# The second FFN product of batches 2 to 7 as seven block products per group, by one level of Strassen's scheme

## Chip, cores, metric

The kernel runs on one core of a Trainium2 chip. The metric is the device time of one execution in microseconds (us).

## What is computed

The reference is a state exchange (an attention between 512 tokens and 32 states, in both directions) followed by a feed-forward network (FFN). Everything is float32.

```python
# x [8, 8, 512, 64], state [8, 8, 32, 64]
scores = scale * x @ state^T;   a  = softmax(scores)     # per batch and head
xread  = a @ state                                       # 512 rows per batch
scores2 = scale * state @ x^T;  a2 = softmax(scores2)
sread  = a2 @ x                                          # 32 rows per batch
y = concat([xread, sread], axis=2) -> [8 * 544, 512]     # heads side by side
h = y @ w_in                                             # [4352, 2048]
g = where(h >= 1, h, where(h <= -1, 0, (h + 1)**2 / 4))
out = g @ w_out                                          # [4352, 512]
```

## The kernel before

**Three passes for one product.** TensorE takes float32 operands here in a rounded form (fp32r). To keep the precision, each operand is split in a rounded high part and a low rest, and each product is made of three matmuls: high by high, high by low, low by high. The split costs one ACT instruction (the rounding copy) and one DVE instruction (the subtraction) for every 128x1024 tile.

**Stages of a batch.** A batch has 512 tokens. Its scores are 16 small matmuls (`scores`, L246), its softmaxes run on DVE and ACT (`second` L392, `first` L401, `halves` L410, called in program order), `trade` (L219) turns the second softmax's layout by way of DRAM on SP's queue, and `read2` (L365) makes the state rows. `a @ state @ w_in` is taken as `a @ (state @ w_in)`: `sw_pair` (L425) makes state by w_in for a 256-wide chunk of the hidden layer, and splits the result. Then come 8 units j per batch, each 256 of the 2048 hidden columns:

- `g1` (L527): the first FFN product, 12 matmuls of 128x512 (L492 to L494), into PSUM tile `h`; then the activation on ACT (`relu` L499, `square` L503) and DVE (`bound` L507), and the split of the hidden values in `gh` (ACT, L519) and `gl` (DVE, L525).
- `g2` (L538): the second FFN product, 24 matmuls of 128x512 (L556 to L558). A tile of `gh` or `gl` (128 hidden by 128 tokens) is the stationary operand, 512 columns of w_out (`wo`, high and low, resident in SBUF) the moving one; four PSUM banks `acc` collect 4 x 128 tokens over all 8 units. `store` (L564) copies them out on ACT and sends them from ACT's queue.

So a batch has 8 x (12 + 24) = 288 matmuls of 512 columns. A ninth, shorter pass (b == B) takes the 256 state rows of all batches through the same FFN.

**Order.** Batch 0, the loading and joining of the weights and a part of batch 1 are put in an order by hand: class `Plan` (L37) holds costs and dependences, the string `ORDER` gives the order of all engines, and `emit` writes it out. From batch 1 on the loop over `steps` (L838) writes the program in the order unit j's `g1`, then a part of the `g2` of unit j - 1 (`cut`, L854), then pieces of the next batch's attention, then the rest of that `g2`; each engine takes its instructions in that order.

## Time and profile before

| | |
|---|---|
| median of 3 runs | 640.94 us (640.75 to 642.06) |
| span of the profiled execution, first to last instruction | 639.1 us |
| TensorE (PE) busy | 631.2 us, 99% |
| DVE busy | 347.2 us, 54% |
| ACT busy | 355.7 us, 56% |
| DMA, mean | 83 GB/s, 53.07 MB |

The page gives the span of the profiled execution and no other time of it. PE is TensorE's matmuls, PEld its weight loads, DVE VectorE, ACT ScalarE, SP the engine that issues most DMAs. Matmuls overlap in their records: one of 512 columns is shown with 0.39 us though the next begins earlier, so the pace is read from starts, not from durations. The same holds for DVE and ACT by about 0.1 us. "<-" behind idle time names what ended it.

### The profile page before, as it was taken

What the parts mean: (1) busy time and instruction counts of PE and PEld (TensorE: products, weight loads), DVE (VectorE), ACT (ScalarE), POOL (GpSimd) and SP (SyncE); (2) the same over time, 40 slices, a digit from 0 to 9 for tenths busy, and PEclk for the clock granted to TensorE, in tenths of its full rate; (3) what the DMA queues carried; (4) which work ended last, traced back from release to release, by engine and by line L of the source; (5) the groups of instructions that cost most, each with busy time, mean ns of one, the idle gap of its engine ahead of it and who ended that gap; (6) DMA issues with size and microseconds to landing.
All of it is one profiled execution on the core that took longest, in us unless ns stands there. A gap on an engine that the chain in (4) does not pass through costs nothing.

```text
span 639.1 us, 10131 instructions
## 1 busy us (share of the span) xinstructions
PE 631.2 (99%) x4298; PEld 505.1 (79%) x4298; DVE 347.2 (54%) x494; ACT 355.7 (56%) x468; POOL 0.8 (0%) x7
## 2 busy tenths in 40 slices
PE   8999999999999999999999999999999999999997
PEld 3677787888787887888787878888787878788896
DVE  6999969433673339433773349332773244333432
ACT  6999767444654457444654456444654454544632
POOL 0000000000000000000000000000000000000000
PEclk9999999999999999999999999999999999999999
DMA  8995245000330015000420015000230012000101
GB/s 357 419 382 224 67 165 198 0 3 0 146 120 1 1 66 199 1 2 1 165 99 1 1 66 199 0 1 1 99 99 1 0 68 66 1 1 1 66 1 33
DMA packets 18476, 53.07 MB, mean 83 GB/s; under 512 B 2048, under 2 KB 7808, under 8 KB 15360
## 3 DMA queue, kind: packets, MB, share of 16 engines
q1 hardware_dynamic: 13488, 43.72, 18.4%
q10 hardware_dynamic: 4944, 8.72, 3.7%
q8 instruction: 33, 0.54, 0.3%
q14 instruction: 11, 0.09, 0.0%
HBM read 38.80 MB, written 13.63 MB: 82 GB/s over the span
## 4 chain that ended last, share of the span: by engine, by line
PE 93%; DMA 3%; DVE 1%; ACT 1%; issue 0%; SPq 0%; ACTq 0%
PE acc L556 19%; PE acc L557 19%; PE acc L558 19%; PE h L492 10%; PE h L493 10%; PE h L494 10%; PE sw L435 4%; DMA raw_o<-in_moe_w_out_dram 2%; PE sr L373 1%; DMA raw_i<-in_moe_w_in_dram 1%; PE sc L264 1%; DVE sw_3l L451 0%; DVE s L297 0%; DVE sw_1l L451 0%; ACT raw_i L602 0%
## 5 line engine op out<-in xcount | busy, mean ns | idle before, releaser
L556 PE MATMUL acc<-wo,gh 128*128 128x512 f32 x544 | 212.9, 391 | 0.0
L557 PE MATMUL acc<-wo,gh 128*128 128x512 f32 x544 | 212.0, 390 | 0.0
L558 PE MATMUL acc<-wo,gl 128*128 128x512 f32 x544 | 211.8, 389 | 0.0
L501 ACT ACTIVATE u<-h,half 128x512 f32<-128x512 f32 (+1 forms) x129 | 91.9, 712 | 174.7 <-PE h L494 163.5
L509 DVE SCALAR_TENSOR_TENSOR u<-u,h 128x512 f32<-128x512 f32 (+1 forms) x129 | 86.6, 710 | 181.2 <-ACT u L505 181.1
L556 PEld LDWEIGHTS acc<-wo,gh 128*128 128x128 f32 x544 | 102.1, 188 | 24.9 <-issue 3.3
L558 PEld LDWEIGHTS acc<-wo,gl 128*128 128x128 f32 x544 | 102.1, 188 | 21.4
L557 PEld LDWEIGHTS acc<-wo,gh 128*128 128x128 f32 x544 | 102.1, 188 | 21.0 <-DVE wo L629 0.2
L525 DVE TENSOR_TENSOR gl<-u,gh 128x1024 fp32r<-128x1024 f32 (+1 forms) x69 | 83.4, 1209 | 53.9 <-ACT gh L519 53.9
L519 ACT CAST gh<-u 128x1024 fp32r<-128x1024 f32 (+1 forms) x69 | 71.6, 1037 | 66.4 <-DVE u L509 65.3
L505 ACT ACTIVATE u<-u 128x1024 f32<-128x1024 f32 (+1 forms) x69 | 72.4, 1049 | 1.8
L435 PE MATMUL sw<-w,sb 64*32 64x256 f32 x1024 | 32.3, 380 | 1.4 <-DVE w L618 1.0
L435 PEld LDWEIGHTS sw<-w,sb 64*32 64x32 f32 x1024 | 18.1, 106 | 10.8 <-DVE u L509 2.1
L571 ACT COPY o<-acc 128x512 f32<-128x512 f32 x33 | 19.0, 583 | 12.1 <-PE acc L558 12.1
L492 PE MATMUL h<-ath,sw_5h 128*128 128x512 f32 x64 | 25.1, 391 | 0.0
L492 PE MATMUL h<-ath,sw_3h 128*128 128x512 f32 x64 | 25.0, 390 | 0.0
L493 PE MATMUL h<-ath,sw_5l 128*128 128x512 f32 x64 | 24.9, 390 | 0.0
L494 PE MATMUL h<-atl,sw_3h 128*128 128x512 f32 x64 | 24.9, 390 | 0.0
L493 PE MATMUL h<-ath,sw_3l 128*128 128x512 f32 x64 | 24.9, 389 | 0.0
L494 PE MATMUL h<-atl,sw_5h 128*128 128x512 f32 x64 | 24.9, 389 | 0.0
L492 PE MATMUL h<-ath,sw_1h 128*128 128x512 f32 x60 | 24.4, 407 | 0.0
L493 PE MATMUL h<-ath,sw_1l 128*128 128x512 f32 x60 | 23.4, 391 | 0.0
(163 smaller groups left out, 693.1 us busy)
## 6 DMA issues: line engine op xcount, KB each, us to landing
xt<-in_xt_dram SPq DMA_DIRECT2D x16, 512.0 KB, 4.2
raw_i<-in_moe_w_in_dram SPq DMA_DIRECT2D x8, 1024.0 KB, 10.7
raw_o<-in_moe_w_out_dram SPq DMA_DIRECT2D x8, 1024.0 KB, 14.7
xn<-in_x_dram SPq DMA_DIRECT2D x8, 1024.0 KB, 5.8
out_dram<-o ACTq DMA_DIRECT2D x32, 256.0 KB, 2.0
e_x<-e_there SPq DMA_DIRECT2D x32, 128.0 KB, 2.9
e_there<-e SPq DMA_DIRECT2D x7, 512.0 KB, 2.6
e_there<-e SPq DMA_DIRECT2D x2, 256.0 KB, 2.8
```

The source lines that it names most:

```text
L435: nc.tensor.matmul(banks[hh][pr * NS:(pr + 1) * NS, cols], lhsT=sb[rows, b, pr], rhs=w32[c][rows, pr], start=True, stop=True,)
L492: nc.tensor.matmul(o, lhsT=wh[:, k, sl], rhs=ah[:, k], start=first, stop=False)
L493: nc.tensor.matmul(o, lhsT=wl[:, k, sl], rhs=ah[:, k], start=False, stop=False)
L494: nc.tensor.matmul(o, lhsT=wh[:, k, sl], rhs=al[:, k], start=False, stop=last)
L501: nc.scalar.activation(out=u, in_=h, func=AF.Relu, scale=0.5, bias=half)
L505: nc.scalar.activation(out=u, in_=u, func=AF.Square)
L509: nc.vector.scalar_tensor_tensor(out=u, in0=u, scalar=1.0, in1=h, op0=ALU.min, op1=ALU.max)
L519: nc.scalar.copy(out=gh, in_=u)
L525: nc.vector.tensor_tensor(out=gl, in0=u, in1=gh.bitcast(F32), op=ALU.subtract)
L556: nc.tensor.matmul(a, lhsT=lh, rhs=oh, start=f == 0, stop=False)
L557: nc.tensor.matmul(a, lhsT=lh, rhs=ol, start=False, stop=False)
L558: nc.tensor.matmul(a, lhsT=ll, rhs=oh, start=False, stop=f == NF - 1)
```

## The change

Batches 0 and 1 and the state rows keep the second product as it was. Batches 2 to 7 are taken in three pairs, and the second product of a pair is made in two groups, one for each half (1024) of the hidden columns: six groups g = 0 to 5. In a group the product is `out^T = w^T g`, with the weights as stationary operand and 512 tokens as moving one. The operands are cut in 2 x 2 blocks: the weights in two halves of the 512 output columns and two interleaved halves of the hidden columns, the hidden values in the two interleaved halves and the two batches of the pair. By one level of Strassen's scheme (in Winograd's form) seven block products k = 1 to 7 take the place of eight. One block product is four `quarter`s of 6 matmuls of 128x512, so a group has 168 matmuls where it had 192.

The scheme needs sums of blocks:

- **Sums of weights.** `block_ops(c)`, for each of 8 chunks: DVE makes the whole weight from its parts and four sums, ACT and DVE split the sums, and SP writes the four plain and the four summed blocks (1 MB each) to DRAM. `weight_ops(g, k)` loads the block of one product (1 MB, in pieces of 1 KB) from DRAM to SBUF; there are two such buffers ("wt"), and 7 loads in each of six groups.
- **Sums of hidden values.** `operand_ops(g, k, half)`: DVE makes the sum in place (T, for k = 5, 6, 7, 4), then ACT and DVE split the operand in `hi` and `lo`, in one of three buffers ("win"). Two operand tiles per product, 14 per group, where there were 8 splits in two half batches.
- **Sums of results.** `done_ops`: a product's PSUM pair is copied (ACT) or added (DVE) into an SBUF tile. Two chains of products go on in PSUM (A: k = 1, 6, 7, 4; B: k = 5, 3), and the next product of the chain waits for the copy. Odd groups add to the result of the even group before and send it, transposed, from SP's queue. The host turns the rows of batches 2 to 7 back (`_rows`).

The loop over `steps` is gone. A second planner, class `Flow`, takes every step from batch 1's first unit on with a cost and dependences; PE's order is written out in the program, and the order on ACT, DVE and SP is made by list scheduling (the step that can begin first, of those the one due first). A whole hidden unit is one `bound` instead of two. PSUM is one tensor of four two-bank pairs, dealt out by the planner; most large SBUF tiles are slots at fixed addresses. The last two `g2` units of batch 1 are put between the first units of batch 2. At the end, the state rows' pass reads w_out back from DRAM (`last_weights`), 8 loads of 1 MB.

The diff, cut to its core (the `Flow` class and the allocation are left out):

```diff
@@
+        flow.kinds.update({kd: ("pair", n) for kd, n in (("base", 6), ("win", 3), ("wt", 2), ("out", 2), ("wo", 8), ("g10", 1), ("spare", 1))})
...
+        flow.kinds.update({kd: ("pb", n) for kd, n in (("h", 4), ("sw", 4), ("sc", 4), ("sr", 4), ("acc", 4), ("A", 1), ("B", 1))})
...
+            op(("dA", c), "SP", 2.6, lambda: store_block(0, rounded(wo_at[c]).bitcast(F32)), [("wol", c)], ends=[("wo", c)])
+            op(("wa", c), "DVE", 1.14, whole, [("wol", c), ("send", 0, 3)], take=[("s", ("s", c))], ends=[("wo", c)])
+            op(("ws", c), "DVE", 1.5, sums, [("wa", c)])
+            op(("wsh", c), "ACT", 0.97, sum_high, [("ws", c)])
+            op(("wsl", c), "DVE", 1.14, sum_low, [("wsh", c)])
+            op(("dS", c), "SP", 2.6, lambda: store_block(1, place()), [("wsl", c)], ends=[("s", c), "spare", "spare2"])
...
+        BLOCK = {1: 0, 2: 2, 3: 7, 4: 3, 5: 4, 6: 5, 7: 6}
+        HOME = {1: (0, 0), 2: (0, 1), 3: (1, 1), 4: (1, 0), 5: (1, 0), 6: (1, 0), 7: (0, 0)}
+        CHAIN = {1: "A", 6: "A", 7: "A", 4: "A", 5: "B", 3: "B", 2: "C"}
...
+            if k == 5:
+                op(("T", g, 1, half), "DVE", 1.14, lambda: tt(s2(), s2(), s1(), ALU.subtract),
+                   blocks_of[homes[0]] + blocks_of[homes[1]])
+                need = [("T", g, 1, half)]
...
+            op(("hi", g, k, half), "ACT", 0.97, lambda: nc.scalar.copy(out=view()[:, 0], in_=value()), need,
+               take=[("win", win)], ends=ends)
+            op(("lo", g, k, half), "DVE", 1.14,
+               lambda: tt(view()[:, 1], value(), view()[:, 0].bitcast(F32), ALU.subtract), [("hi", g, k, half)], ends=ends)
...
+                part, n = divmod(BLOCK[k], 4)
+                nc.sync.dma_start(
+                    out=rounded(flow.place[h]).bitcast(F32).rearrange("p (c f) -> p c f", f=CI),
+                    in_=blocks[g % 2, part].rearrange("p c (e k f) -> p (c e) k f", e=2, k=4)[:, :, n],
+                )
...
+            op(h, "SP", 2.6, fetch_block, [("dA" if BLOCK[k] < 4 else "dS", 4 * (g % 2) + c) for c in range(4)],
+               take=[("wt", h)])
...
+        def quarter(g, k, n):
...
+                for d in range(2):
+                    o = chain(g, k)[:, d]
+                    wh, wl = (w[:, n, e, d * P:(d + 1) * P] for e in range(2))
+                    for m, (lhs, e) in enumerate(((wh, 0), (wl, 0), (wh, 1))):
+                        nc.tensor.matmul(
+                            o, lhsT=lhs, rhs=v[:, e, a], start=fresh and n == m == 0, stop=n == 3 and m == 2,
+                            skip_group_check=not fresh,
+                        )
...
+            if n == 0 and k in (6, 7, 3, 4):
+                need.append(({6: "X", 7: "Y", 3: "V", 4: "C22"}[k], g))
...
+            add = odd or name in ("C12", "C22", "C11")
...
+                if add:
+                    nc.vector.tensor_tensor(out=c, in0=c, in1=src, op=ALU.add)
+                else:
+                    nc.scalar.copy(out=c, in_=src)
...
+        for j, (k, n) in enumerate(((1, 0), (1, 2), (2, 0), (2, 2))):
+            step(0, k, n)
+            step(0, k, n + 1)
+            unit_ops(3, j)
+        for g in range(5):
+            b, j0 = 2 + (g + 1) // 2 * 2, 4 * ((g + 1) % 2)
+            both(b, j0)
+            read_ops(3 + g)
+            if 4 + g < B:
+                score_ops(4 + g)
+            ks = (5, 6, 3, 7, 4) if g == 0 else (1, 5, 6, 3, 7, 2, 4)
+            places = (0, 3, 5, 8, 10, 13, 16, 18) if g == 0 else (2, 5, 9, 12, 16, 19, 23, 26)
+            middle = 9 if g == 0 else 14
+            line = [(k, n) for k in ks for n in range(4)]
+            for n in range(len(line) + 1):
+                if n in places:
+                    i = places.index(n)
+                    unit_ops(b + i // 4, j0 + i % 4)
+                if n == middle:
+                    both(b + 1, j0)
+                if n < len(line):
+                    step(g, *line[n])
+        sread_ops()
+        line = [(k, n) for k in (1, 5, 6, 3, 7, 2, 4) for n in range(4)]
+        for n, q in enumerate(line):
+            if n in (16, 22):
+                last_unit((16, 22).index(n))
+            step(5, *q)
```

Here `unit_ops` is the first product and activation of one unit, `both` makes two `sw_pair`s of two chunks each, `read_ops` is `read2`, `score_ops` is the attention of one batch, and `step` is `weight_ops`, `operand_ops` and `quarter` of a product's quarter n.

## Rows read from the trace of the kernel before

**Rows 1.** The page's head and busy times (us, share of the span, instructions).

```profile
span 639.1 us, 10131 instructions
PE 631.2 (99%) x4298; PEld 505.1 (79%) x4298; DVE 347.2 (54%) x494; ACT 355.7 (56%) x468; POOL 0.8 (0%) x7
```

**Rows 2.** The page's chain that ended last, by engine.

```profile
PE 93%; DMA 3%; DVE 1%; ACT 1%; issue 0%; SPq 0%; ACTq 0%
```

**Rows 3.** The same chain in order of time: start us, us, what.

```profile
165.25 1.03 PE sr L373 x64
166.28 1.89 PE sw L435 x64
168.17 0.86 PE sc L264 x16
...
236.68 1.03 PE sr L373 x64
```

**Rows 4.** Timeline of PE: start us, us, line, out<-in, shapes.

```profile
171.13 0.39 PE L492 MATMUL h<-ath,sw_1h 128*128 128x512 f32 x1
...
171.81 0.39 PE L556 MATMUL acc<-wo,gh 128*128 128x512 f32 x1
...
177.25 0.39 PE L492 MATMUL h<-ath,sw_1h 128*128 128x512 f32 x1
```

**Rows 5.** Windows, one batch: PE, PEld, DVE, ACT, POOL busy; clock; DMA share; GB/s.

```profile
236.68:308.11 71.43, 71.43 (x500) 57.52 (x504) 36.57 (x56) 37.40 (x51) 0.00 (x0) 1.00 0.17 60
```

**Rows 6.** Timeline of DVE while it runs without a break.

```profile
49.08 1.22 DVE L618 SCALAR_TENSOR_TENSOR w<-raw_i 128x1024 int32<-128x1024 int32 x1
50.21 0.68 DVE L284 TENSOR_REDUCE m<-z 128x16 f32<-128x512 f32 x1
50.81 1.22 DVE L525 TENSOR_TENSOR gl<-u,gh 128x1024 fp32r<-128x1024 f32 x1
```

**Rows 7.** Timeline of ACT while it runs without a break.

```profile
39.56 1.03 ACT L519 CAST gh<-u 128x1024 fp32r<-128x1024 f32 x1
40.50 1.05 ACT L625 CAST wo<-wf 128x1024 fp32r<-128x1024 f32 x1
```

**Rows 8.** Windows of 20 us: two of the stage with a list schedule, one later.

```profile
40.00:60.00 20.00, 20.00 (x116) 15.76 (x115) 19.19 (x23) 19.94 (x23) 0.00 (x0) 1.00 0.83 316
60.00:80.00 20.00, 20.00 (x117) 15.93 (x116) 19.50 (x25) 16.11 (x20) 0.00 (x0) 1.00 0.18 53
...
240.00:260.00 20.00, 20.00 (x99) 16.25 (x87) 18.33 (x33) 12.20 (x20) 0.00 (x0) 1.00 0.46 159
```

**Rows 9.** The page's DMA issues: KB each, us to landing.

```profile
raw_i<-in_moe_w_in_dram SPq DMA_DIRECT2D x8, 1024.0 KB, 10.7
raw_o<-in_moe_w_out_dram SPq DMA_DIRECT2D x8, 1024.0 KB, 14.7
xn<-in_x_dram SPq DMA_DIRECT2D x8, 1024.0 KB, 5.8
...
e_x<-e_there SPq DMA_DIRECT2D x32, 128.0 KB, 2.9
e_there<-e SPq DMA_DIRECT2D x7, 512.0 KB, 2.6
```

**Rows 10.** Windows of 1 us: a trade's reads in 1 KB pieces, then xn.

```profile
250.00:251.00 1.00, 1.00 (x6) 0.81 (x6) 0.96 (x3) 0.22 (x1) 0.00 (x0) 1.00 0.87 264
251.00:252.00 1.00, 1.00 (x6) 0.84 (x5) 0.97 (x3) 0.86 (x2) 0.00 (x0) 1.00 0.94 215
...
253.00:254.00 1.00, 1.00 (x6) 0.84 (x5) 1.00 (x3) 1.00 (x3) 0.00 (x0) 1.00 1.05 418
```

**Rows 11.** Timeline of PE, first stage: waits in brackets.

```profile
13.29 0.67 PE L435 MATMUL sw<-w,sb 64*32 64x256 f32 x16 [0.99 <-DVE w L618]
...
17.41 0.67 PE L435 MATMUL sw<-w,sb 64*32 64x256 f32 x16 [0.45 <-DVE sw_0l L451]
```

**Rows 12.** Timeline of DVE: the kernel's last compute instruction.

```profile
635.07 0.69 DVE L569 COPY o<-acc 128x512 f32<-128x512 f32 x1 [5.42 <-PE acc L558]
```

More of the change, by code (lines that the diff above doesn't have):

```diff
@@ L18 @@
 WARM = 7
-PAD = 120
+PAD = 96
+UNITS = 27
 EARLY = (2, 3)
@@ L263, in scores @@
                         m = m[:, half]
[L264 to L266 removed]
+                    nc.tensor.matmul(o, lhsT=sb[rows, b, pr], rhs=m, start=True, stop=True)
         def tokens(self, half):
@@ L918, in _laid_out, with _rows @@
     }
+def _rows(y):
+    y = y.copy()
+    for b in range(2, 8):
+        y[b * 544:b * 544 + 512] = y[b * 544:b * 544 + 512].T
+    return y
 def kernel(**inputs):
```

782 lines of the change are left out of this document (611 added, 171 removed).

## Prediction

> **What bounds the kernel now.** The first look is at the busy times and the span [rows 1]: TensorE (PE) is busy for 631.2 of 639.1 us, the other engines for a little over half of it. A busy PE need not be at its pace, so the second look is at the chain that ended last [rows 2, 3]: 93% of it is PE, and in the steady batches it goes from one PE instruction to the next, with nothing between. The third is at the starts on PE's timeline [rows 4]: a `g2` unit of 24 matmuls runs from 171.81 to 177.25, so 5.44 / 24 = 0.2267 us each, and the `g1` matmuls ahead of it keep the same pace (0.68 / 3). The fourth is at a batch [rows 5]: 71.43 us from one `read2` to the next [rows 3], PE without a gap at clock 1.00, DVE 36.57 us and ACT 37.40 us. The sum agrees: 288 x 0.2267 + 1.03 + 1.89 + 1.89 + 0.86 [rows 3] = 70.96, and 0.47 us for the changes between kinds of matmul. So every PE instruction that goes is worth its full pace, as long as nothing else comes to be late; DVE has 35 us free in each batch, ACT 34.
>
> **What is removed.** Each of the six groups has 24 matmuls of 128x512 fewer: 144 x 0.2267 = 32.6 us. The new ones have the shape and the operand kinds of `g1` (128x128 stationary, 512 moving), whose pace is the same [rows 4]. The median, 640.94, stands 1.84 us above the span, and no other time of that execution is shown; I leave those 1.84 us as they are and make the sum on the median: 640.94 - 32.64 = 608.3 us, if PE never waits. The first stage (up to unit 0 of batch 1) and the tail behind PE (a 0.69 us copy and a DMA, 639.1 - 635.07 = 4.0 us [rows 12]) stay. The Trainium skill ("TensorE: Matmul & The Clock Gate", in "Wait — 56ns, not 53.3ns?") has a warm matmul start every N / 2.4 GHz plus 2.5 ns, 215.8 ns here, by which the gain would be 31.1 us. The trace disagrees for these fp32r matmuls, and its 226.7 ns is what I use.
>
> **What DVE gets.** DVE's price is read from starts too: behind a 128x1024 instruction the next begins after 1.13 us, behind a 512 one after 0.60 [rows 6]. A batch period of before becomes one turn of the loop over g, with 65.99 us of PE (71.43 - 5.44). DVE's 36.57 us get 8 sums T and 6 more `lo` splits, and result adds: 7 in an odd group, 3 in an even one. Loops 1 and 3: 36.57 + 21 x 1.13 = 60.3 us, 91% of 65.99. Loop 2: 17 more, 55.8 us, 85%. Loop 0 has only 20 quarters (20 x 1.36 + 8 x 2.72 + 6.14 = 55.1 us of PE) and 12 more instructions, 50.1 us, 91%. Loop 4 has no attention and lies well below. The weight sums lie in batch 1's stage of some 115 us: 8 chunks x (2 x 1.13 + four quarter-size sums). Four of those cost between one full instruction (1.13) and four half ones (2.4); I take 1.5, so 30 us (27 to 37), on top of 0.51 x 115 = 59 us. DVE is under 85% there, and they cost nothing. The merged `bound` saves under 0.1 us each and is left out. ACT: 6 more roundings and up to 4 copies at 0.94 us [rows 7], less four output copies: under 47 us of 65.99. It doesn't bind.
>
> So DVE is nowhere over 100%, and the question is whether 91% can be filled without PE waiting. One stretch of the trace shows it: the stage that is already in a list-scheduled order has DVE at 19.19 and 19.50 of 20 us (ACT at 19.94 in the first), and PE at 20.00 in both [rows 8]. The operands have slack as well. An operand's buffer comes free three tiles ahead, four quarters and a unit (8.16 us) before its use, and making it takes 0.94 + 1.13 us and two hand-overs. I take nothing for DVE's load as such.
>
> **PSUM pairs.** At the start of a turn two `sw_pair`s, `read2`, scores and the fresh chain A take five pairs in 3.8 us, where four exist. The first to come back is the first `sw_pair`'s, 0.95 + 0.94 + 1.13 us and three hand-overs after its start, some 3.3 us if DVE is free at once and 4.5 if it has just begun another 1024 instruction. Chain A then waits between 0 and 1.2 us. The two `sw_pair`s in the middle of a turn meet a like squeeze. Ten places x 0 to 1.2 us: 0 to 12; I take 0.25 each, 2.5 us, since in several of the ten the last hidden unit's pair is back in time.
>
> **The weight stream.** A load of 1 MB begins when the product before the last frees its buffer, and must land within one product. Pieces of 1 KB ran at 264 GB/s with the DMA engines 0.87 busy and at 215 with 0.94 [rows 10], so 303 to 215 GB/s at full use, 3.5 to 4.9 us. To this comes the fixed part: `e_there`, 512 KB in 2.6 us, leaves 1.35 us beyond its 1.25 at 418 GB/s; `xn`, 1 MB in 5.8, leaves 3.3, but stands behind `e_x` [rows 9, 10]. Bounds 4.8 to 8.2 us. I take 5.7 (240 GB/s and 1.35), since a load whose buffer has just come free is alone as `e_there` is. In loops 0 to 4 a product has at least one hidden unit beside its four quarters: 5.44 + 2.72 = 8.16 us, so the load is hidden. In group 5 three products (k = 5, 6, 3) have 5.44 us alone: 3 x 0.3 = 0.9 us (0 to 8.3). The output DMAs go from ACT's queue to SP's, and the trades, `xt` and `xn` share SP's queue with the loads. A load that waits there for its buffer holds them back, but what they feed (`kept`, `read2`, the next scores) is used a turn later. The 16 stores of 1 MB lie in batch 1, where the DMA engines are 0.17 busy over a batch [rows 5]. The eight loads of w_out at the end have buffers freed 10 us or more before their use, at nothing.
>
> **Sum.** 608.3 + 2.5 + 0.9 = 611.7 us. Its own range: 608 to 619.
>
> **The rivals.**
>
> *DVE becomes the bound.* In the loop that was written by hand DVE's best stretch is 18.33 of 20 us [rows 8]; a full turn at 91% with chains DVE - ACT - DVE in it is not in the trace, and rows 8 stand for 40 us, not 250. If DVE can be filled to only 0.85, loops 0, 1 and 3 take 58.9, 70.9 and 70.9 us: 13.6 us more than PE's, 625 us. If it is under 0.80, the four loops take 226.5 / 0.80 = 283 us against PE's 253.1, and the whole gain is gone: that is the case on the other side, slower than before, and 0.80 is where it decides (0.75 gives 661 us).
>
> *The weights come late.* With a load of L us, loops 1 to 4 pay 28 x (L - 9.43) and group 5 7 x (L - 7.0); the forecast's gain of 29.2 us is gone at L = 9.8. For it: in the first stage 1 MB took 10.7 to 14.7 us [rows 9], and 10.7 gives 61 us more, 673 us. Against it: there many loads stood in one queue with the DMA engines 0.83 busy and more [rows 8]. The Trainium skill ("DMA: Bandwidth & Descriptors", "Latency and other measured facts") says that copies between HBM tensors whose partitions lie a large power of two apart run at 103 to 207 GB/s, from a pitch of 512 KiB up. The stored blocks have a pitch of 32 KiB, which it does not list; no run here shows it yet. At its 103 GB/s, an estimate, a load would take 11.5 us, and this rival would be the outcome.
>
> *The planner's waits aren't the program's.* With one PSUM tensor and overlapping SBUF views, waits may be written between steps that don't touch the same bytes, and PE would wait before each quarter. In the first stage a `sw_pair` waited for its operand 0.45 to 0.99 us [rows 11]; 168 quarters x 0.45 = 76 us, 688 us, and 0.17 us per quarter takes the gain. Nothing in the steady rows shows such a wait.
>
> **How the numbers follow.** Forecast (608 to 619 us) 0.62. DVE at 0.80 to 0.89 (619 to 640 us) 0.22, most of it below 630. DVE below 0.80, 0.05; late weights, 0.05; waits at the quarters, 0.05: all slower. Within 0.2%, which is about what a measurement of this kernel can tell from no change, 0.01. So faster 0.84, same 0.01, slower 0.15. The range 608 to 630 leaves out the slower cases and the end of the DVE case, 0.2 in all.
>
> **What would show it.** 4154 or so matmuls, with starts 0.2267 us apart in the quarters. One turn of loops 1 to 3 in 66 to 67 us, PE at 19.8 or more of 20, DVE at 17 to 18. Waits of PE at the starts of turns, on DVE's `sw` split or the last result, up to 1 us each. In group 5 PE waits of some 0.3 us on DMA, at products 5, 6 and 3. Weight loads landing in 5 to 7 us. The clock stays 1.00. Wrong it is if PE's waits are on `lo`, T or a result add through the whole of loops 0 to 3 (DVE), on the weight loads (stream), or before quarters whose operands have long been there (waits). If PE's pace in the quarters is not 0.2267 us, the first step fails.

## The result, and the profile after

The changed kernel takes **620.58 us** (median of 4 runs, 619.43 to 621.72) against 640.88 (640.75 to 642.06) for the kernel before: a ratio of 0.968, with a 95% interval of 0.9666 to 0.9694. The forecast was 611.7 us with a range of 608 to 630. So the direction and the range held, but 8.9 us of the gain that was forecast didn't come, and this part is about where they went.

The head of the page of after and its chain by engine (compare [rows 1, 2]):

```profile
span 618.8 us, 10012 instructions
PE 602.2 (97%) x4154; PEld 477.1 (77%) x4154; DVE 497.5 (80%) x574; ACT 391.3 (63%) x480; POOL 0.8 (0%) x7
...
PE 82%; DVE 10%; DMA 4%; ACT 3%; issue 1%; SPq 0%; DVEq 0%
```

There are 144 matmuls fewer, as said. In the profiled executions the sum of the prediction gives a span of 639.1 - 32.64 = 606.5 us if PE never waits; the span is 618.8. So 12.3 us were lost, where the prediction had put 3.4. The chain that ended last has 10% of DVE in it where it had 1%: PE waits for DVE somewhere. The windows by stage say where (length; PE, PEld, DVE, ACT, POOL busy; clock; DMA share; GB/s). The first is batch 1's stage, then come loop 0 and the turns of loops 1 to 3:

```profile
84.30:208.50 124.20, 119.06 (x920) 92.64 (x918) 102.77 (x141) 77.51 (x103) 0.00 (x0) 0.99 0.66 246
208.54:267.42 58.88, 55.69 (x425) 43.66 (x424) 49.70 (x57) 41.23 (x52) 0.00 (x0) 1.00 0.43 143
267.42:333.58 66.16, 66.16 (x474) 52.85 (x473) 57.70 (x65) 41.14 (x52) 0.00 (x0) 1.00 0.57 183
333.58:399.73 66.15, 66.15 (x473) 52.84 (x473) 55.99 (x63) 42.95 (x54) 0.00 (x0) 1.00 0.51 168
399.73:465.88 66.15, 66.15 (x473) 52.84 (x472) 57.70 (x65) 41.26 (x52) 0.00 (x0) 1.00 0.53 168
```

The turns of loops 1 to 3 run as forecast: 66.15 us each (65.99 forecast), PE without a gap though DVE is 85 to 87% busy. Batch 1's stage and loop 0 don't: PE is idle for 5.1 and 3.2 us there. The prediction had put the first at nothing and the second's share at half a microsecond. The waits themselves stand in brackets on PE's timeline (start us, us, instruction, idle before and what ended it). These are all of them from batch 1's stage on:

```profile
95.89 1.09 PE L455 MATMUL bank<-xt,sb 64*32 64x512 f32 x16 [0.54 <-DVE sw_1l L621]
129.02 0.67 PE L605 MATMUL bank<-w,sb 64*32 64x256 f32 x16 [0.88 <-DVE one L681]
134.16 0.50 PE L664 MATMUL bank<-ath,sw_5h 128*128 128x512 f32 x1 [0.50 <-DVE sw_7l L621]
154.23 1.96 PE L605 MATMUL bank<-w,sb 64*32 64x256 f32 x32 [2.43 <-DVE sw_0l L621]
186.56 3.02 PE L1261 MATMUL bank<-r,r 128*128 128x512 f32 x12 [0.80 <-DVE f L681]
211.74 1.10 PE L569 MATMUL bank<-xn,one 128*32 128x64 f32 x64 [1.24 <-DVE f L681]
215.14 0.50 PE L664 MATMUL bank<-ath,sw_4h 128*128 128x512 f32 x1 [1.17 <-DVE sw_6l L621]
240.33 1.10 PE L605 MATMUL bank<-w,sb 64*32 64x256 f32 x32 [0.74 <-DVE f L681]
500.41 1.10 PE L605 MATMUL bank<-w,sb 64*32 64x256 f32 x32 [0.36 <-DVE f L681]
```

They add up to 8.66 us: 5.15 in the stage, 3.15 in loop 0, 0.36 in loop 4. In eight of the nine the waiting work is one of the small products (`sw_pair` at L605, `read2` at L569, scores at L455) or the first matmul of a hidden unit (L664) behind small products. No quarter in loops 1 to 4 or in group 5 waits.

The longest wait can be followed step by step on three engines: PE's first `sw_pair`, ACT's rounding, DVE's subtraction, PE's second `sw_pair`.

```profile
150.70 1.09 PE L605 MATMUL bank<-w,sb 64*32 64x256 f32 x32
...
151.91 1.01 ACT L619 CAST sw_0h<-bank 128x1024 fp32r<-128x1024 f32 x1 [0.17 <-PE bank L605]
...
152.95 1.23 DVE L621 TENSOR_TENSOR sw_0l<-bank,sw_0h 128x1024 fp32r<-128x1024 f32 x1 [0.53 <-ACT sw_0h L619]
```

One PSUM pair goes through the whole chain before the second `sw_pair` can begin at 154.23: 3.53 us from start to start. The prediction had priced this chain at 3.3 us, but saw a need for it at the starts and middles of turns alone. Here two `sw_pair`s stand back to back in PE's order while four banks still collect batch 1's output, so that of the four pairs only two are dealt out to everything else, and one of these was in use.

Behind this wait PE was slow as well. Windows of 1 us, with the granted clock as the third number from the right:

```profile
154.00:155.00 1.00, 0.77 (x16) 0.45 (x24) 0.70 (x2) 1.00 (x2) 0.00 (x0) 0.60 0.00 0
155.00:156.00 1.00, 1.00 (x24) 0.22 (x8) 1.00 (x2) 0.40 (x1) 0.00 (x0) 0.50 0.00 0
156.00:157.00 1.00, 1.00 (x10) 0.79 (x3) 0.83 (x1) 0.70 (x1) 0.00 (x0) 0.50 0.60 254
157.00:158.00 1.00, 1.00 (x4) 0.76 (x4) 0.66 (x1) 0.31 (x1) 0.00 (x0) 0.69 0.95 401
```

The clock fell to 0.50, the lower of its two levels (1.2 of 2.4 GHz), and came back by 158. The `sw_pair` of 154.23 took 1.89 us to the next matmul where others take 1.02, and the four matmuls from 156.12 to 157.83 took 1.71 where four take 0.91: 1.67 us more. Waits and low clock together are 10.3 of the 12.3 us.

Of the DMA groups the new ones are (KB each, us to landing; compare [rows 9]):

```profile
r<-blocks SPq DMA_DIRECT2D x50, 1024.0 KB, 5.5
...
blocks<-r SPq DMA_DIRECT2D x8, 1024.0 KB, 10.5
```

A weight load lands in 5.5 us (5.7 forecast). The stores of plain blocks take 10.5.

### The profile page after: what moved, and what is told of

It is laid out like the page before. It is cut to its first block, busy times and chain, and to the rows that moved or that the text cites. A ratio compares the mean times of both kernels' runs of the same rounds, so it can differ in the third digit from the quotient of the medians.

```text
span 618.8 us, 10012 instructions
## 1 busy us (share of the span) xinstructions
PE 602.2 (97%) x4154; PEld 477.1 (77%) x4154; DVE 497.5 (80%) x574; ACT 391.3 (63%) x480; POOL 0.8 (0%) x7
## 3 DMA queue, kind: packets, MB, share of 16 engines
q1 hardware_dynamic: 65040, 121.32, 55.8%
## 4 chain that ended last, share of the span: by engine, by line
PE 82%; DVE 10%; DMA 4%; ACT 3%; issue 1%; SPq 0%; DVEq 0%
PE bank L1261 37%; PE bank L664 9%; PE bank L666 9%; PE bank L665 9%; PE bank L717 4%; PE bank L719 4%; PE bank L718 4%; PE bank L605 3%; DMA blocks<-f 1%; DMA f<-in_moe_w_in_dram 1%; DMA e_there<-one 1%; DVE one L681 1%; DVE w L778 1%; PE bank L455 1%; PE bank L569 1%; DVE r L696 1%
## 5 line engine op out<-in xcount | busy, mean ns | idle before, releaser
L1261 PE MATMUL bank<-r,r 128*128 128x512 f32 x1008 | 238.9, 391 | 0.8 <-DVE f L681 0.8
L1261 PEld LDWEIGHTS bank<-r,r 128*128 128x128 f32 x1008 | 188.4, 188 | 44.6 <-issue 2.1
L673 ACT ACTIVATE f<-bank,half 128x512 f32<-128x512 f32 x104 | 71.7, 689 | 107.2 <-PE bank L666 106.4
L1203 DVE TENSOR_TENSOR r<-f,r 128x1024 fp32r<-128x1024 f32 x84 | 101.6, 1218 | 9.1 <-ACT r L1227 8.9
L1227 ACT CAST r<-f 128x1024 fp32r<-128x1024 f32 x84 | 87.0, 1046 | 27.6 <-PE bank L1261 13.4
L681 DVE SCALAR_TENSOR_TENSOR f<-f,bank 128x1024 f32<-128x1024 f32 x52 | 63.2, 1216 | 38.1 <-ACT f L677 37.8
L717 PE MATMUL bank<-r,r 128*128 128x512 f32 x160 | 63.1, 395 | 0.0
L718 PE MATMUL bank<-r,r 128*128 128x512 f32 x160 | 62.6, 391 | 0.0
L719 PE MATMUL bank<-r,r 128*128 128x512 f32 x160 | 62.6, 391 | 0.0
L677 ACT ACTIVATE f<-f 128x1024 f32<-128x1024 f32 x52 | 55.2, 1061 | 1.3
L1295 DVE TENSOR_TENSOR one<-one,bank 128x1024 f32<-128x1024 f32 x30 | 36.4, 1214 | 14.5 <-PE bank L1261 14.5
L1203 DVE TENSOR_TENSOR f<-f,f 128x1024 f32<-128x1024 f32 x36 | 43.3, 1216 | 0.0
L605 PE MATMUL bank<-w,sb 64*32 64x256 f32 x1024 | 34.0, 388 | 5.9 <-DVE sw_0l L621 2.9
L717 PEld LDWEIGHTS bank<-r,r 128*128 128x128 f32 x160 | 30.3, 189 | 8.5 <-issue 1.2
L719 PEld LDWEIGHTS bank<-r,r 128*128 128x128 f32 x160 | 30.2, 189 | 6.4
L718 PEld LDWEIGHTS bank<-r,r 128*128 128x128 f32 x160 | 30.2, 189 | 6.1
L605 PEld LDWEIGHTS bank<-w,sb 64*32 64x32 f32 x1024 | 17.3, 108 | 19.3 <-issue 4.6
L681 DVE SCALAR_TENSOR_TENSOR one<-one,bank 128x1024 f32<-128x1024 f32 (+1 forms) x17 | 19.6, 1155 | 2.3 <-ACT one L677 2.2
L664 PE MATMUL bank<-ath,sw_0h 128*128 128x512 f32 x52 | 20.5, 394 | 0.0
## 6 DMA issues: line engine op xcount, KB each, us to landing
blocks<-r SPq DMA_DIRECT2D x8, 1024.0 KB, 10.5
```

The source lines that it names most:

```text
L605: nc.tensor.matmul(banks[hh][pr * NS:(pr + 1) * NS, cols], lhsT=sb[rows, b, pr], rhs=w32[c][rows, pr], start=True, stop=True,)
L664: nc.tensor.matmul(o, lhsT=wh[:, k, sl], rhs=ah[:, k], start=first, stop=False)
L673: nc.scalar.activation(out=u, in_=h, func=AF.Relu, scale=0.5, bias=half)
L681: nc.vector.scalar_tensor_tensor(out=u, in0=u, scalar=1.0, in1=h, op0=ALU.min, op1=ALU.max)
L717: nc.tensor.matmul(a, lhsT=lh, rhs=oh, start=f == 0, stop=False)
L718: nc.tensor.matmul(a, lhsT=lh, rhs=ol, start=False, stop=False)
```

## The experiments

All times are medians of 4 runs, each beside runs of the kernel before on the same chip (medians of 640.75 to 640.88 us).

### Why PE waits in batch 1's stage and in loop 0

Three theories. **A**: small products ask for a PSUM pair before one is back, because of their place in PE's order. **B**: DVE is overfull with the sums of weights. **C**: DVE stands for a buffer that is still being stored, and what is queued behind it comes late.

**The sums left out.**

```diff
+            def both_stores():
+                for first in range(2):
+                    store_block(first, rounded(wo_at[c]).bitcast(F32))
-            op(("dA", c), "SP", 2.6, lambda: store_block(0, rounded(wo_at[c]).bitcast(F32)), [("wol", c)], ends=[("wo", c)])
-            op(("wa", c), "DVE", 1.14, whole, [("wol", c), ("send", 0, 3)], take=[("s", ("s", c))], ends=[("wo", c)])
-            op(("ws", c), "DVE", 1.5, sums, [("wa", c)])
+            op(("dA", c), "SP", 2.6, both_stores, [("wol", c)], ends=[("wo", c)])
+            op(("wa", c), "DVE", 1.14, lambda: None, [("wol", c), ("send", 0, 3)], take=[("s", ("s", c))], ends=[("wo", c)])
+            op(("ws", c), "DVE", 1.5, lambda: None, [("wa", c)])
...
```

> Left out: DVE's and ACT's instructions for the sums of the weights (some 30 us of DVE in batch 1's stage); the second set of stores sends the plain weights again, so DRAM traffic and all orders stay. The changed kernel stands 12.3 us above the sum of PE's work, 8 to 9 of it in batch 1's stage (84 to 209 us), 3 to 4 in loop 0, in eight waits of PE at the small products (state by w_in, scores, read2), the longest 2.43 us at 151.8 us with the clock at its lower level behind it. Theory A (these products ask for a pair of PSUM banks before one is back, because of where they stand in PE's order): the waits shrink where a late DVE held the pair, but don't go: 614 to 618 us. Theory B (DVE is overfull with the sums): the waits of batch 1's stage go, 611 to 613 us. Theory C (DVE stands still for the stores, as at 121.7 us for 3.4 us, and is late from there on): without sums nothing waits for a store, so also 611 to 613 us; the next run tells B from C.

Measured: 621.54 us (620.93 to 622.53), ratio 0.9702 (0.9687 to 0.9716). Nothing was gained. The window with the longest wait, and the wait on PE's timeline:

```profile
140.00:160.00 20.00, 17.57 (x128) 13.26 (x127) 7.85 (x7) 10.53 (x12) 0.00 (x0) 0.94 0.32 121
```

```profile
157.01 1.39 PE L605 MATMUL bank<-w,sb 64*32 64x256 f32 x32 [2.43 <-DVE sw_0l L621]
```

DVE is busy for 7.85 of 20 us here, and the wait is 2.43 us as before, to the hundredth. An engine that is free for 60% of the time isn't overfull: B falls. The waits of 0.50, 0.80 and 0.88 us went, but the 16 stores now come as soon as the weights are split, and a trade waits behind them (DVE's timeline, then PE's):

```profile
122.81 1.25 DVE L551 STREAM_TRANSPOSE one<-e_x 128x1024 f32<-128x1024 f32 x1 [8.70 <-DMA e_x<-e_there]
...
126.56 0.50 PE L717 MATMUL bank<-r,r 128*128 128x512 f32 x1 [2.15 <-ACT r L690]
```

What was gained at the small waits was lost at 126 us, and the clock fell to 0.50 behind this wait as well. The sums of weights had spread the stores out.

**Half of the stores left out.**

```diff
-            op(("dS", c), "SP", 2.6, lambda: store_block(1, place()), [("wsl", c)], ends=[("s", c), "spare", "spare2"])
+            op(("dS", c), "SP", 2.6, lambda: None, [("wsl", c)], ends=[("s", c), "spare", "spare2"])
...
-                part, n = divmod(BLOCK[k], 4)
+                part, n = 0, BLOCK[k] % 4
```

> Left out: the eight stores of the summed weights (8 of 16 MB); the loads of summed blocks read plain blocks in the same pieces. DVE's and ACT's work and all orders stay. Theory C: DVE no longer stands still for 3.4 us for a buffer that is being stored, and the waits of batch 1's stage go: 611 to 614 us. Theory B: DVE has the same work, no change beyond 2 us: 618 to 621 us. Theory A: as B, at most 2 to 3 us less where the late DVE held a pair: 617 to 621 us.

Measured: 618.66 us (617.62 to 619.97), ratio 0.9662 (0.9646 to 0.9678), 1.9 us below the changed kernel. The waits of 0.88, 0.50 and 0.80 us (2.2 together) are gone and one of 0.49 has come; the 2.43 us and all of loop 0's stay. So C is right for about 2 us, and no more. In the changed kernel it is seen on DVE's timeline:

```profile
125.02 1.23 DVE L1167 TENSOR_TENSOR f<-r 128x1024 f32<-128x1024 f32 x1 [3.36 <-DMA blocks<-f]
```

DVE's next instruction in its queue, a whole-weight sum, waits 3.36 us for a store to leave its buffer, and the `bound` queued behind it hands back its pair late (L681 on DVE ends the 0.88 us of 129.02).

**Only two lines of PE's order.**

```diff
         unit_ops(1, 7)
-        g2_half(1, 5, 0)
         sw_make((2, 0), (2, 1))
-        sw_make((2, 2), (2, 3))
+        g2_half(1, 5, 0)
         g2_half(1, 5, 1)
+        sw_make((2, 2), (2, 3))
         unit_ops(2, 0)
```

> All work as in the changed kernel; only two lines of PE's order in batch 1's stage change places: the first sw_pair of batch 2 goes one half unit earlier, the second one half unit later, so that they no longer stand back to back. Theory A (a sw_pair asks for its PSUM pair before ACT and DVE have handed one back, because of its place): the 2.43 us wait at 154 us goes, and a new one of at most 0.4 us at another place comes; 620.6 - 2.4 + 0.4 = 618.6 us if the lower clock behind that wait (0.50 to 0.60 from 154 to 157 us) stays, and 1.3 to 1.8 us less, 617 us, if the low clock is a consequence of the wait. Theory D (the low clock at 154 us has another cause, such as the DMA load of that stretch): the low clock stays near 154 us in the windows of 1 us. Theory C (DVE stands for the stores): the waits come back elsewhere in the stage, and the time stays at 620 to 621 us.

Measured: 617.79 us (615.6 to 618.34), ratio 0.9632 (0.9614 to 0.9651). A window, and a wait on PE's timeline:

```profile
140.00:160.00 20.00, 20.00 (x143) 15.33 (x142) 19.86 (x26) 14.79 (x17) 0.00 (x0) 1.00 0.44 186
```

```profile
131.03 0.67 PE L605 MATMUL bank<-w,sb 64*32 64x256 f32 x16 [2.79 <-DVE one L681]
```

The 2.43 us wait is gone without another in its neighbourhood, with DVE at 19.86 of 20 us, and the clock is 1.00: with the wait, the low clock is gone. The DMA load, which theory D named, isn't its cause: with the sums left out the clock fell behind the same wait while no DMA ran.

```profile
158.00:159.00 1.00, 1.00 (x10) 0.58 (x3) 0.63 (x1) 0.55 (x1) 0.00 (x0) 0.50 0.00 0
```

But the wait doesn't always bring the clock down. With half of the stores left out the same 2.43 us are followed by a clock of 1.00, and from this `sw_pair` to the next matmul 1.02 us pass, not 1.89:

```profile
153.03 1.10 PE L605 MATMUL bank<-w,sb 64*32 64x256 f32 x32 [2.43 <-DVE sw_0l L621]
```

```profile
153.00:154.00 1.00, 0.97 (x32) 0.50 (x32) 0.73 (x1) 1.00 (x2) 0.00 (x0) 1.00 0.00 0
```

The wait of 0.80 us at 186 went as well. What wasn't expected is the row of 131.03: the wait that had been 0.88 us at 129 is 2.79 here. The planner had put DVE's and SP's steps in another order even before 131 us, and DVE stood 5.27 us for a store where it had stood 3.36. By the rows: 2.43 + 1.67 + 0.80 saved, 1.91 given back, 3.0; measured 2.8.

**The small products moved apart in the whole stage.** Work and planner are unchanged. Lines of PE's order change places, the lines of `block_ops` come to stand between them, and the planner orders ACT, DVE and SP anew (the first lines of the edit):

```diff
-        unit_ops(1, 0)
-        for n in range(2):
-            g2_half(0, 7, n)
-        for c in range(NC):
-            block_ops(c)
         sw_make((1, 1), (1, 2))
-        sw_make((1, 3), (1, 4))
-        read_ops(0)
+        unit_ops(1, 0)
+        g2_half(0, 7, 0)
+        g2_half(0, 7, 1)
+        block_ops(0)
+        block_ops(1)
+        block_ops(2)
         score_ops(2)
...
```

> Only PE's order in batch 1's stage (84 to 209 us) is changed: the same small products (state by w_in, read2, scores) stand apart from one another, between the halves of the big products. DVE, ACT and DMA have the same work, list-scheduled by the same rule. Theory A: the waits of that stage go, and the lower clock with them: 611 to 614 us; loop 0 keeps its waits. Theories B and C: the work of DVE and the stores are what they were, so 617 to 621 us.

Measured: 616.06 us (615.83 to 616.56), ratio 0.9616 (0.9601 to 0.963), 4.5 us below the changed kernel. Of the stage's 5.15 us of waits 0.38 is left, and the clock is 1.00 throughout.

**The same in loop 0 as well.** In the order of loop 0 `read2` goes first, the two middle `sw_pair`s stand apart and two units go elsewhere:

```diff
+            if g == 0:
+                read_ops(3)
+                sw_make((2, 4), (2, 5))
+                sw_make((2, 6), (2, 7))
+                score_ops(4)
+                unit_ops(2, 4)
...
+                sw_make((3, 4), (3, 5))
+                unit_ops(2, 7)
...
+                sw_make((3, 6), (3, 7))
...
```

> As e4_moved_stage, and the small products of loop 0 are moved apart in the same way. Theory A: loop 0's 3 to 4 us go too, 608 to 611 us, PE's work being 608.3 us by the sum. Theories B and C: 616 to 621 us.

Measured: **614.15 us** (613.33 to 614.75), ratio 0.9584 (0.957 to 0.9598), 6.4 us below the changed kernel. These waits are left:

```profile
134.56 0.50 PE L664 MATMUL bank<-ath,sw_5h 128*128 128x512 f32 x1 [1.60 <-DVE sw_5l L621]
...
208.08 1.09 PE L455 MATMUL bank<-xt,sb 64*32 64x512 f32 x16 [0.21 <-DVE f L681]
209.44 0.50 PE L664 MATMUL bank<-ath,sw_4h 128*128 128x512 f32 x1 [0.27 <-DVE sw_4l L621]
...
494.27 1.10 PE L605 MATMUL bank<-w,sb 64*32 64x256 f32 x32 [0.36 <-DVE f L681]
```

So A is shown for the larger part: with no work taken away and only the order changed, 6.2 of the 8.66 us of waits and the low clock go. Of the stage's waits up to 2.2 us can be put down to C as well, since they also went when stores were left out. The 2.43 us, which two lines removed, and loop 0, whose waits stayed when stores were left out, are A's alone.

### How much DVE can take

The prediction's first rival was that DVE can't be filled to 91% without PE waiting. The turns of 66.15 us say that it can; how far it goes is measured by giving DVE more work.

**Half of each `lo` split done twice, and the whole of it.**

```diff
-            op(("lo", g, k, half), "DVE", 1.14,
-               lambda: tt(view()[:, 1], value(), view()[:, 0].bitcast(F32), ALU.subtract), [("hi", g, k, half)], ends=ends)
+            def low():
+                tt(view()[:, 1], value(), view()[:, 0].bitcast(F32), ALU.subtract)
+                tt(view()[:, 1, 0], value()[:, 0], view()[:, 0, 0].bitcast(F32), ALU.subtract)
+
+            op(("lo", g, k, half), "DVE", 1.14, low, [("hi", g, k, half)], ends=ends)
```

> Nothing is left out; behind each of the 14 lo splits of a group DVE repeats one half of it (128x512, 0.60 us), 8.4 us more of DVE in a group, at nothing for PE. In the three full turns DVE was busy 57.70, 55.99 and 57.70 of 66.15 us; now it has 66.1, 64.4 and 66.1. Theory F (DVE's share costs nothing up to 100%): the turns stay within 0.5 us of 66.15, and the whole within 2 us of 620.6. Rival G (a loop with chains between DVE and ACT can be filled to 95% only): turns of 69.6, 67.8 and 69.6 us, 8.5 us more, 629 us. Rival H (the prediction's rival, 0.85 to 0.87): turns of 76, 74 and 76 us, 648 us.

> Nothing is left out; DVE does each of the 14 lo splits of a group twice (128x1024, 1.13 us), 15.8 us more of DVE in a group: 73.5, 71.8 and 73.5 us of DVE work for turns in which PE has 66.15. Theory F (only what is over 100% costs): the turns take DVE's time, 73.5, 71.8 and 73.5 us, 20.4 us more; loop 0 (49.7 us of DVE in 58.9, 11 to 14 more) 2 to 4 us more; group 5 and loop 4 up to 5 us more: 643 to 650 us, slower than before. Theory G (95%): turns of 77.4, 75.6 and 77.4 us, 32 us for these alone, 655 us and more. If PE's time doesn't follow DVE's, 630 us or less, then what is queued on DVE isn't what PE waits for.

Measured: 645.18 us (643.85 to 645.34) with the half repeats, 24.6 us more than the changed kernel and 0.6% above the kernel before (ratio 1.0061, 1.0046 to 1.0076); 667.87 us (667.05 to 671.16) with the full ones, 47 us more. F falls as it was put: with the half repeats the first full turn takes 71.54 us, though DVE is busy for only 67.11 of them. A turn has two halves, divided by its second pair of `sw_pair`s. The changed kernel's first full turn in halves, then the same with the half repeats, cut at the same `sw_pair`, and PE's wait behind the cut:

```profile
267.42:301.50 34.08, 34.08 (x277) 26.98 (x276) 33.40 (x42) 22.00 (x30) 0.00 (x0) 1.00 0.59 186
301.50:333.58 32.08, 32.08 (x198) 25.87 (x197) 24.30 (x24) 19.14 (x22) 0.00 (x0) 1.00 0.55 181
```

```profile
273.24:308.02 34.78, 34.17 (x277) 26.96 (x276) 34.47 (x45) 20.59 (x29) 0.00 (x0) 1.00 0.56 182
308.02:344.78 36.76, 33.85 (x197) 26.60 (x197) 32.64 (x35) 20.79 (x24) 0.00 (x0) 0.95 0.48 154
```

```profile
312.03 1.47 PE L605 MATMUL bank<-w,sb 64*32 64x256 f32 x32 [2.91 <-DVE f L681]
```

In the changed kernel DVE is busy for 33.40 of 34.08 us in the first half, 98%, and for 76% of the second: the mean of 87% hid a half with 0.7 us to spare. On DVE's timeline seven of the 14 splits of the turn stand in the first half, so the half repeats add 7 x 0.60 = 4.2 us to it, 3.5 more than there was room for. PE's waits up to the second `sw_pair` behind the cut are 0.61 and 2.91 us, 3.52 together: DVE is busy for 99% of the time up to the cut, its queue runs on behind it, and that `sw_pair` stands for a pair whose `bound` comes late in the queue. The rest of the 5.38 us by which the turn grew lies behind this wait, where the clock fell to 0.50.

**Six repeats in the second half only.** New theory K: each half is a unit of its own.

```diff
+            def low():
+                again = g in (1, 2, 3) and k in (2, 4) or g in (2, 3, 4) and k == 1
+                for _ in range(2 if again else 1):
+                    tt(view()[:, 1], value(), view()[:, 0].bitcast(F32), ALU.subtract)
```

> Nothing is left out; DVE repeats six lo splits (128x1024, 1.13 us) in each of loops 1 to 3, those that fall into the second half of a turn (products 2 and 4, and product 1 of the next group): 6.8 us more of DVE in a turn, against the 8.4 us of the half repeats, which were spread over the whole turn and made a turn 5.4 to 5.9 us longer. In the changed kernel DVE had 33.40 of 34.08 us in the first half of a turn (up to its second pair of sw_pairs) and 24.30 of 32.08 in the second; now it has 33.4 and 31.1. Theory K (each half of a turn is a unit of its own: the sw_pairs between them wait for DVE's queue, so that DVE's work costs nothing up to 100% of a half and its full time beyond): turns within 0.5 us of 66.15 and 620.6 us for the whole, though DVE is busy 64.5 of 66.15 us, 97%. Rival G (DVE can be filled to a share of a whole turn only, 92% by the half repeats: 66.1 of 71.5 us): 64.5 / 0.92 = 70.1 us for a turn, 12 us more in three turns, 632 us.

Measured: 620.81 us (619.53 to 621.57), ratio 0.9684 (0.9669 to 0.9699): no change.

```profile
268.33:302.41 34.08, 34.08 (x277) 26.97 (x276) 33.40 (x42) 22.00 (x30) 0.00 (x0) 1.00 0.56 186
302.41:334.49 32.08, 32.08 (x197) 25.85 (x196) 31.61 (x30) 19.14 (x22) 0.00 (x0) 1.00 0.51 159
```

DVE is busy for 65.01 of 66.16 us, 98% of the turn, and PE never waits. K holds and G falls: 6.8 us of DVE work cost nothing in one half of the turn, while 8.4 us spread over both cost 5.4 to 5.9 us a turn.

### The weight stream

```diff
-                nc.sync.dma_start(
-                    out=rounded(flow.place[h]).bitcast(F32).rearrange("p (c f) -> p c f", f=CI),
-                    in_=blocks[g % 2, part].rearrange("p c (e k f) -> p (c e) k f", e=2, k=4)[:, :, n],
-                )
+                for _ in range(2):
+                    nc.sync.dma_start(
+                        out=rounded(flow.place[h]).bitcast(F32).rearrange("p (c f) -> p c f", f=CI),
+                        in_=blocks[g % 2, part].rearrange("p c (e k f) -> p (c e) k f", e=2, k=4)[:, :, n],
+                    )
```

> Nothing is left out; each 1 MB weight load is issued twice into the same buffer by SP, one behind the other, so that a product's weights are there only when 2 MB have landed. One load took 5.5 us to landing; the second adds 2.5 (418 GB/s) to 4.9 us (215 GB/s): 8.0 to 10.4 us. Theory S (the stream was hidden, with what a product takes as its margin: 8.16 us and more in loops 1 to 4, 5.44 to 9.4 us in group 5): the turns stay at 66.2 us if the load takes under 8.2 us, and group 5 loses 7 x (L - 7.0), 7 to 24 us; 628 to 645 us, with PE waits on the weight buffer in group 5. Rival W (late weights already cost something in the loops): the turns grow by 7 x (L - 9.43) only above L = 9.43, so with L = 10.4 by 6.8 us each, 28 us more in the loops as well. If neither grows, the real margin is larger than the formulas of the prediction have it: the load then starts earlier than when the product before the last ends.

Measured: 717.97 us (716.76 to 722.87), 97 us more, far outside what was expected. The dose was not the intended one: the second load goes into the same buffer, and SP waits with it until the first has landed. The waits of PE and of SP's queue (us in total, times, longest):

```profile
PE bank L1262 <- DMA r<-blocks: 50.9, 16, 9.3
...
SPq L1238 <- DMA r<-blocks: 321.1, 42, 13.7
```

SP waited 321.1 / 42 = 7.6 us for each first load, and 7.2 us is the page's median for all loads, to landing: together some 14.8 us, not 8.0 to 10.4. So this run shows that late weights would have taken the whole gain, as that rival had it, and not how large the margin is. By the prediction's formula 14.8 us would have cost 7 x (14.8 - 9.43) = 38 us in each turn; the first turns grew from 66.15 to 82.4, 86.1 and 77.8 us, half of that or less. How much later than 5.5 us a load may land stays open.

### What is left

**Another order, with units moved in all loops.** The small products and hidden units stand at other places in the stage and in loops 0 to 4, and most `sw_pair`s stand alone among quarters (some 230 lines of order):

```diff
+        sw_make((4, 2), (4, 3))
+        read_ops(4)
+        step(1, 1, 0)
+        step(1, 1, 1)
+        score_ops(5)
+        sw_make((4, 0), (4, 1))
+        step(1, 1, 2)
...
```

> The same work as in the changed kernel; PE's order is another in batch 1's stage and in loops 0 to 4: the sw_pairs, read2, scores and hidden units stand at other places, apart from each other. Theory A: the waits for PSUM pairs in the stage and in loop 0 (8 us with the lower clock behind them in the changed kernel, of which the order that moved only the small products took 6.4) go but for some 1 us, and the 0.36 us at 500 us too: 612 to 614 us. Theory C (what is left are stands of DVE for stores in batch 1's stage): 1.5 to 3 us of waits stay between 120 and 160 us. If the order with moved units brings operands too late, new waits on lo, T or hi stand in the loops and the time is above 614.2 us.

Measured: 615.59 us (615.47 to 616.06), ratio 0.9606 (0.9592 to 0.9621). The windows of 20 us from batch 1's stage on have PE at 20.00, but for one:

```profile
204.00:224.00 20.00, 19.48 (x191) 14.97 (x180) 19.55 (x23) 14.18 (x19) 0.00 (x0) 1.00 0.67 211
```

That is a wait of 0.52 us, and no other is left in the stage or the loops; none on T, `hi` or `lo` has come. And yet it takes 1.4 us more than the order with 2.4 us of waits, and more than any theory expected. Its span, 613.6 us, is 7 us above 606.5. So there is a cost that no bracket shows.

**The stores given their true length in the plan.** PE's order is that of the 614.15 us kernel.

```diff
-            op(("dS", c), "SP", 2.6, lambda: store_block(1, place()), [("wsl", c)], ends=[("s", c), "spare", "spare2"])
+            op(("dS", c), "SP", 6.5, lambda: store_block(1, place()), [("wsl", c)], ends=[("s", c), "spare", "spare2"])
```

> PE's order of the kernel with the small products moved apart in the stage and in loop 0 (614.15 us), and the planner is told 6.5 us instead of 2.6 for each of the eight stores of summed weights, so that it places DVE's sums behind other work of DVE. Theory C (PE's wait of 1.60 us at 134.56 us in that kernel is DVE's stand for a buffer that is being stored): that wait goes, and the time is 612.5 to 613 us. If DVE stands for another buffer or PE's pairs come late elsewhere by the new order, the time stays at 614 us or rises.

Measured: 613.98 us (613.69 to 617.52), ratio 0.9595 (0.9564 to 0.9626): the same, and a wait of 1.50 us stands where 1.60 stood. The expectation named the wrong buffer. DVE stands here for an output piece of batch 0 that shares the place with the sums, not for a stored sum (in the kernel that it started from, the same stand is 4.65 us):

```profile
126.90 1.23 DVE L1167 TENSOR_TENSOR f<-r 128x1024 f32<-128x1024 f32 x1 [4.12 <-DMA out_dram<-f]
```

**The small products apart where nothing waits.** In loops 1 to 4 the second `sw_pair` of each two goes one quarter later.

```diff
-            both(b, j0)
+            if g:
+                sw_make((b, j0), (b, j0 + 1))
+            else:
+                both(b, j0)
...
+                if n == 1 and g:
+                    sw_make((b, j0 + 2), (b, j0 + 3))
...
```

> The same work; in loops 1 to 4 of the changed kernel, where PE waits nowhere but for 0.36 us at 500 us, the second sw_pair of each two goes one quarter later, so that in each turn two more places stand where PE changes from 512-wide matmuls to a sw_pair's 256-wide ones and back. Theory P (each such place costs PE time without a wait in the trace: from the start of the last three matmuls of a quarter to the sw_pair behind them 0.77 us passed where three take 0.68, so 0.09 us on the way in, and some 0.1 on the way out): turns of 66.15 + 2 x 0.19 = 66.5 us, four of them, less the 0.36 us wait: 621.7 us. This would account for part of the 6 us by which the kernel with the free order (613.6 us span, 0.5 us of waits) stays above the sum. Theory Q (the places cost nothing, and the rest of that kernel's time is something else): turns of 66.15 us and 620.2 us for the whole. If the chain A of a turn waits for the pair of the moved sw_pair, a wait of up to 1 us before a quarter shows it.

Measured: 624.35 us (622.96 to 625.99), ratio 0.9744 (0.9722 to 0.9766), 3.8 us more than the changed kernel. The first full turn, and one of the places on PE's timeline:

```profile
268.94:335.86 66.92, 66.92 (x474) 52.31 (x473) 57.90 (x65) 41.19 (x52) 0.00 (x0) 1.00 0.57 181
```

```profile
272.01 1.67 PE L1261 MATMUL bank<-r,r 128*128 128x512 f32 x6
273.61 1.09 PE L605 MATMUL bank<-w,sb 64*32 64x256 f32 x32
274.64 0.73 PE L1261 MATMUL bank<-r,r 128*128 128x512 f32 x2
```

Each of the three full turns is 66.92 us, 0.77 us longer, with PE busy throughout and no wait: 0.38 us for each of the two new places, twice what theory P had. Four such turns make 3.1 us. The waits of PE come to 9.5 us instead of 8.66, and both together are the 3.9 us by which the spans differ. At the place shown, the `sw_pair` begins 0.09 us later behind the last quarter matmul than another quarter matmul would, its 32 matmuls take 0.09 us more than at 0.0295 each, and the first quarter matmul behind it takes 0.33 us to the next, 0.11 more than the pace. That is 0.28 us; the other 0.1 wasn't found at one spot. P holds, Q falls. This is why taking small products apart has a price, and why the free order gained nothing over the other with fewer waits.

The places can be counted on PE's timeline, as unbroken groups of small products from 84 us on: 14 in the kernel before, 16 in the changed kernel, 24 here, 23 in the kernel of 614.15 us, 34 in the free order. The free order has 18 more than the changed kernel, and its span leaves 613.6 - 618.8 + 8.14 + 1.67 = 4.6 us for them when the waits and the low clock that went are added back: 0.26 us each, so 0.38 isn't the price of every place. The changed kernel's two more than before are 0.5 to 0.8 of its last 2 us; the rest wasn't separated.

## Why the prediction was right or wrong, point by point

The sum's own range, 608 to 619 us, was missed by 1.6 us. 620.58 lies in the band of 619 to 640 us that was set aside for a DVE filled beyond what it can take, and that isn't what happened. So the stated range of 608 to 630 held the result partly by luck: room that was left for one mechanism was used by others.

- **144 matmuls at 0.2267 us: right.** 108 quarter matmuls of group 5 run in 24.48 us of the chain, 0.2267 each (a piece of the chain in order of time; behind it DVE's last instruction on its timeline). The turn measured 66.15 us where the sum had 65.99; the tail is 618.8 - 614.64 = 4.2 us, 4.0 before [rows 12].

```profile
528.93 24.48 PE bank L1261 x108
```

```profile
614.64 0.69 DVE L733 COPY one<-bank 128x512 f32<-128x512 f32 x1 [10.97 <-PE bank L719]
```

- **DVE's load as such costs nothing: right, by less than it looked.** DVE was busy for 57.70 and 55.99 us a turn (60.3 and 55.8 in the sum). The rival that DVE can be filled to 0.85 only is refuted: 98% of a turn cost nothing when the work lay in the right half. But the share of a whole turn was the wrong number to read, and so was the rival's point of decision at 0.80. The first half stood at 98%, and 4.2 us more in it, with the clock that fell behind the waits, turned the result into a loss. The prediction had no view of the changed kernel's halves, but it could have counted the work by halves.

- **Batch 1's stage at nothing: wrong, and the largest error.** The step argued from DVE's share ("DVE is under 85% there, and they cost nothing"). The share was 102.77 of 124.20 us, 83%, and without the sums 58%; the wait of 2.43 us was there either way. A mean share of DVE says nothing of a chain in which PE, ACT and DVE take turns.

- **PSUM pairs: mechanism and price right, places wrong.** The prediction had 3.3 us for a pair to come back; the trace has 3.53. But it looked for the squeeze at ten places in loops 0 to 4 and took 0.25 us each. Loops 1 to 4, eight of them, cost 0.36 us together. Loop 0's two cost 3.15 us: its start alone has two waits of 1.2 us. The bound of 1.2 us for a place was a slip besides: a pair back after 4.5 us and asked for after 3.8 leaves 0.7. Batch 1's stage, with two pairs in place of four, wasn't counted at all and cost 5.15. The term of 2.5 us should have been 8.7, stands for stores included, and moving the small products took most of it away.

- **The clock stays at 1.00: wrong for 4 us of the profiled execution.** A wait that PE spent between two `sw_pair`s was followed by matmuls at half rate, 1.67 us. So a wait can cost more than its length. It needn't: the same wait was followed by 1.00 where half of the stores were left out, and one of the changed kernel's four runs has a mean clock of 1.000 and a span of 617.5 us, 1.0 to 2.3 below the others.

- **The weight stream: right.** 5.5 us to landing against 5.7, and no wait for it in group 5, where 0.9 us had been taken. The Trainium skill ("DMA: Bandwidth & Descriptors", "Latency and other measured facts") has copies between HBM tensors at 103 to 207 GB/s where partitions lie a large power of two apart, from 512 KiB up. At 103 a load would have been 11.5 us, by an estimate; the trace has half of that, so at this pitch of 32 KiB, which the Trainium skill doesn't list, its slow case didn't appear. One bound of the sum was off: 215 GB/s with the engines 0.94 busy are 229 at full use, so 4.6 us and not 4.9. Nothing hung on it.

- **Stores at nothing: wrong by 2 us.** The argument was that the DMA engines are free. They were busy to 0.66 in the stage, and to 0.93 from 100 to 120 us; the cost came by way of buffers: DVE's queue stood 3.36 us for one that was being stored.

- **Changes between kinds of matmul: not in the sum.** They were seen in the rows of before (0.47 us a batch) and taken as unchanged. A further place costs 0.26 to 0.38 us, and the changed kernel has two more than before.

The account: 606.5 us, waits of 5.15 in the stage, 3.15 in loop 0 and 0.36 later, and 1.67 of low clock make 616.8; the span is 618.8, and the 2 us between are the changes of kind (0.5 to 0.8 us) and what wasn't separated. Against the forecast that is 6.2 us more of waits, 1.7 of low clock and 2.0 of the rest, less the 0.9 that the weight stream didn't take.

## What to carry to other kernels

Count PSUM buffers along PE's order, stage by stage, with the time in which one comes back (here 3.5 us through ACT and DVE): two small products back to back cost the return time less their own length (2.43 us here) where only one buffer is free, and a change of place in PE's order alone was worth 6.4 us here. Read an off-path engine's share between the points at which PE waits for its queue, not over a whole turn: 87% of a turn was 98% of one half, with 0.7 us to spare. But keep small products together where buffers allow it, since each further change between them and the large ones cost 0.3 to 0.4 us that no wait shows.

## What the runs showed of the hardware that was not expected

- The granted clock fell to 0.50 behind the wait of 2.43 us between two `sw_pair`s of 32 matmuls in the changed kernel. With the sums left out it fell behind the same wait, and behind one of 2.15 us between 512-wide matmuls (0.50 from 127 to 130 us). It stayed at 1.00 behind the same 2.43 us with half of the stores left out, and behind a longer wait of 2.79 us, which was followed by a `sw_pair` of 16 and then by 512-wide matmuls:

```profile
130.00:131.00 1.00, 0.00 (x0) 0.00 (x0) 1.00 (x2) 0.92 (x1) 0.00 (x0) 1.00 0.91 282
131.00:132.00 1.00, 0.97 (x18) 0.52 (x19) 1.00 (x1) 0.99 (x2) 0.00 (x0) 1.00 0.99 304
```

  These are windows of the kernel with two lines exchanged. So in these runs neither the length of a wait nor the matmuls on either side of it decide by themselves; what does stays open. The Trainium skill ("TensorE: Matmul & The Clock Gate", "HAM oscillation — how this bites in real kernels") describes a kernel in which waits between bursts of matmuls bring the clock down, so that the next burst starts slow. The trace of the changed kernel agrees with that; in the two other runs the waits of 2.43 and 2.79 us left the clock at 1.00.
- A `sw_pair` between two quarters cost 0.38 us beside its own matmuls in the turns of one run, and 0.26 us on average in the free order. At the one place followed row by row, 0.09 us stands before its first matmul, 0.09 within and behind its own, and 0.11 behind the first 512-wide matmul after it; why wasn't looked into.
- With all 16 stores issued early (408 GB/s), a trade's reads made DVE stand 8.70 us; with the stores spread out by DVE's sums (346 GB/s from 100 to 120 us), DVE's longest stand for a DMA in the stage was 3.36 us.
